# A recurrent layer with a gated feed-forward product: a chunk's state update and scores issued as one run of small matmuls, and a new order for the first 42 products

## The chip, the cores and the metric

The kernel runs on one core of a Trainium2 chip. The metric is the device time of one execution in microseconds (us). A difference is written as a share of the time before.

## The reference

The inputs are r, k, v, w of 4 batches, 8 heads, 768 steps and 48 values per head, a vector u per head, and two weight matrices of 384 x 2048 and 2048 x 384.

```
state = 0                                       # 48 x 48 per batch and head
for t in 768 steps:
    cur   = k[t] (outer) v[t]
    y[t]  = r[t] @ (state + u * cur)
    state = w[t] * state + cur
x   = y as 3072 tokens x 384
h   = x @ w_in
out = (h * sigmoid(1.702 h)) @ w_out
```

## The kernel before, in words

**The recurrence** is worked in 24 chunks of 128 steps, six to a batch, all eight heads at once. Heads stand in pairs: one head of a pair on partitions 0 to 47, the other on 64 to 111, four pairs along the free axis. A chunk is a generator, `chunk(t)`; each `yield` ends a piece, and the order of pieces is set outside. Its pieces before are, with the tiles that they write:

1. S1, S2: two scans of the decay on VectorE (L229, L235, tile `lp`), and the product r*k (`rku`);
2. KQ: decayed keys and queries (L250, L251, tile `kq`);
3. D: for the first eight chunks, matmuls for the u term (`ps_d`, L257); s: its copy, and the old state `sf` scaled (L267);
4. T: the keys transposed on TensorE (`ps_t`, L273) and copied by ScalarE (`kt`, L275); am: the diagonal of the score matrix, eight ScalarE operations (L282);
5. U: the state update. For each half of the chunk, 64 steps, keys times values, 16 small matmuls into two PSUM tiles `ps_u` (L290, L291); VectorE makes from them `mid`, the state at the half (L296; L294 on ScalarE for a batch's first chunk), and the new `sf` (L299). A batch's last chunk needs only the first half;
6. S: the scores, 16 matmuls of keys and queries in blocks of 64 x 64 into two tiles `ps_s`, one for each head of a pair (L306);
7. P: the scores are masked into `am` (L309);
8. Y: scores times values, and half of the state's part (`ps_y`, L319, L330); Z: the other half (L330), and the result split into two f32r halves in `x` (L199, L200). After a group's last chunk, three pairs of small DMAs fill spare rows of `x` (L356).

Each of the 16 matmuls of a piece shows twice in the profile. The tiles `ps_d`, `ps_t`, `ps_u`, `ps_s` and `ps_y` all come from one pool of three PSUM banks, `ps_a`, in turn.

**The feed-forward part** takes four chunks as a group of 512 columns. A task is 128 rows of the hidden layer for a group: a first product g (nine matmuls into `ph`, L368 to L370, the high and low parts of x and w_in), a gelu h (two ScalarE operations L379, L380 and one subtraction `gl` on VectorE, L381), and a second product y (nine matmuls into `po`, L394 to L396). The first group starts before its four chunks are done: its first tasks are cut to 256 columns, chunks 0 and 1 (columns 0 to 2) or 2 and 3 (columns 2 to 4). There are 106 tasks, 86 of them with 512 columns.

**The weights** come in six slices for each matrix; f fetches a slice by DMA, w converts it in four pieces into a high and a low part: two ScalarE operations (L185, L186), two VectorE operations (L188, L191), one on ScalarE (L193), one on VectorE (L195). Even numbers (w0, w2, ...) are slices of w_in (`wih`, `wil`), odd ones of w_out (`woh`, `wol`).

**The order** is written by hand, and every engine takes its instructions in that order. Up to task 42 it stands in the string `RAMP`: a token is a letter (l load, a next piece of a chunk, m a sum of squares on ScalarE, f, w, g, h, y as above, x the fill, u and M small loads) and a number. From task 42 on the list `PARTS` sets it: a row ("a", 4, 1) says that a chunk's next piece stands four tasks after the chunk's beginning, and 0 or 1 says whether it stands before the task's g or between its h and the y of the task two before. Chunks begin four tasks apart.

```python
PARTS = [("a", 0, 0), ("a", 1, 0), ("a", 2, 0), ("m", 2, 0), ("a", 2, 1), ("a", 3, 0), ("m", 3, 0), ("l", 3, 0),
         ("l", 3, 0), ("a", 3, 1), ("a", 4, 0), ("a", 4, 1), ("a", 5, 1), ("a", 5, 1), ("a", 6, 1), ("a", 7, 0), ("x", 7, 0)]
```

Of the kernel before, what the change touches and what calls it, by code (L numbers as in the profile page):

```python
# [14 lines left out]
ALU = mybir.AluOpType  # L15
# [15 lines left out]
NF = DFF // P  # L31
# [28 lines left out]
FIRST = 42
RAMP = """
l0 l1 l0 a0 a0 a0 M a0 a0 l0 m0 a0 a1 a0 a1 a0 f0 l1 a0 a0 f1 a1 m0 a1 a0 w0 a1 a0 a1 l2 m1 w0 a1 f2 a1 w1 a1
a2 a1 a2 a1 l3 a2 w0 m1 a1 m2 a2 w0 a2 a2 x1 w1 m2 a3 w2 w2 w1 g0 a3 a2 h0 f3 w1 g1 l2 a3 w2 m3 a2 w3 a2 f4 l3
w2 g2 a3 w3 a2 a3 h1 m3 h2 w4 f5 g3 a3 a2 w4 a3 a2 y0 y1 w3 a3 a3 f6 g4 a3 w4 w3 a3 w4 w5 a3 h3 l4 y2 h4 w6 g5
y3 x3 w5 h5 y4 g6 w5 w6 f7 g7 w5 h6 a4 h7 g8 l4 w6 g9 a4 f8 y5 h8 y6 w7 y7 h9 g10 w6 y8 h10 y9 w8 g11 g12 a4
w7 h11 h12 w7 y10 w7 g13 y12 a4 f9 h13 w8 g14 y11 a4 l5 w9 h14 f10 w9 m4 a4 y13 g15 a5 g16 h15 a4 y14 f11 a5
h16 g17 w8 w8 y15 g18 l6 h17 a5 w9 h18 y16 a4 w9 g19 g20 w10 l7 a5 h19 y17 w10 m4 a5 a4 y18 w11 w11 l5 y19 m5
h20 w10 a4 w11 g21 w10 a5 a4 w11 h21 a4 a6 a5 a5 m5 y20 a5 g22 l6 a6 a6 y21 m6 a5 a6 h22 a5 a6 a7 a5 a6 a6 y22  # L70
a7 a6 g23 a6 m6 a7 l8 a7 a6 a7 m7 a7 l7 a6 a8 g24 h23 a6 a7 a7 g25 a7 u l8 a8 a7 l9 a8 m7 h24 y23 a7 h25 a7
y24 l9 m8 a8 a8 x7 a9 a9 a9 a8 l10 a8 y25 a8 a9 g26 g27 a8 a9 h26 l10 g28 y26 m8 h27 a9 a8 y27 g29 a8 m9 l11
h28 m9 a8 a9 a10 y28 a9 a10 g30 a9 a9 h29 g31 h30 g32 a10 h31 g33 a9 a9 m10 a10 y29 l11 a10 a11 h32 l12 y30
a10 h33 g34 a11 l12 y31 g35 h34 a11 a10 y32 a11 h35 m10 a10 y33 l13 y34 a10 g36 a10 a11 a10 a10 a11 m11 g37
l13 h36 a12 y35 a12 h37 a11 g38 h38 a11 a11 m11 y36 a12 a11 g39 a12 g40 y37 y38 h39 h40 a11 m12 a11 a12 l14
a12 a13 x11 m12 y39 a12 a12 g41 h41 l14
"""
WIDE = 512
assert sum(CHUNKS) == NT
# [3 lines left out]
def rwkv_ffn_kernel(ctx: ExitStack, tc, wkr, vp, vrk, ub, w_in, w_out, masks, vt, uc, out):  # L83
    nc = tc.nc
    V, A, G, T = nc.vector, nc.scalar, nc.gpsimd, nc.tensor
# [49 lines left out]
    loaded, state, pools = {}, {}, {}  # L135
# [80 lines left out]
    def chunk(t):

        i, col = where[t]
        a, v = loaded[t][:2]
        n, nc_ = NP * CW, NP * C  # L220
        w0, w1 = a[:, 0:n], a[:, 1 : n + 1]
        k = a[:, n + 1 : n + 1 + nc_].rearrange("r (p c) -> r p c", p=NP)
        r = a[:, n + 1 + nc_ :].rearrange("r (p c) -> r p c", p=NP)
        first, final = t % CB == 0, (t + 1) % CB == 0
# [39 lines left out]
        sf = None  # L264
        if not first:
            sf = state[t - 1]
# [15 lines left out]
                A.activation(x_[:, p], same, AF.Copy, scale=s[:, 2 * p + h : 2 * p + h + 1])  # L282
        yield

        blocks = [slice(HB * b, HB * b + HB) for b in range(2)]
        ps = [ps_a.tile([R2, NP, D], F32, tag="psa", name=f"ps_u{b}") for b in range(1 if final else 2)]
        for p in range(NP):
            for b, o in enumerate(ps):

                T.matmul(o[0:HB, p], kt[blocks[b], p, 0:HB], v[blocks[b], 2 * p], start=True, stop=True)  # L290
                T.matmul(o[HB:R2, p], kt[blocks[b], p, HB:R2], v[blocks[b], 2 * p + 1], start=True, stop=True)  # L291
        mid = at.tile([R2, NP, D], F32, tag="mid", name="mid", bufs=2)
        if first:
            A.copy(mid, ps[0])  # L294
        else:
            V.tensor_tensor(mid, ps[0], sf, op=ALU.add)  # L296
        if not final:
            new = state[t] = at.tile([R2, NP, D], F32, tag="sf", name="sf", bufs=2)
            V.tensor_tensor(new, ps[1], mid, op=ALU.add)  # L299
        yield  # L300

        ps = [ps_a.tile([P, NP, HB], F32, tag="psa", name=f"ps_s{h}") for h in range(2)]
        for p in range(NP):
            for b in blocks:
                for h in range(2):
                    T.matmul(ps[h][b, p], kf[head(h), p, b], qf[head(h), p, b], start=True, stop=True)  # L306
# [36 lines left out]
        x = xs[i]  # L343
# [18 lines left out]
    def first_product(j, task):  # L362
        i, c0, c1, f = task
        cs = slice(c0 * C, c1 * C)
        ph = ps_h.tile([P, WIDE], F32, tag="ph", name="ph")[:, 0 : (c1 - c0) * C]
        for c in range(NM):
            h_, l_ = (w[:, f, c * P : (c + 1) * P] for w in (wih, wil))
            T.matmul(ph, h_, xs[i][:, 0, c, cs], start=c == 0, stop=False)  # L368
            T.matmul(ph, h_, xs[i][:, 1, c, cs], start=False, stop=False)  # L369
            T.matmul(ph, l_, xs[i][:, 0, c, cs], start=False, stop=c == NM - 1)  # L370
        parts[j] = ph

    def gelu(j, task):
        i, c0, c1, f = task
        ph, n = parts[j], (c1 - c0) * C
        gf = mo.tile([P, WIDE], F32, tag="gf", name="gf")[:, 0:n]
        gh = mo.tile([P, WIDE], F32R, tag="gh", name="gh", bufs=LAG + 1)[:, 0:n]
        gl = mo.tile([P, WIDE], F32R, tag="gl", name="gl", bufs=LAG + 1)[:, 0:n]
        A.activation(gh, ph, AF.Gelu_apprx_sigmoid, scale=1.0 / W_SCALE)  # L379
        A.activation(gf, ph, AF.Gelu_apprx_sigmoid, scale=1.0 / W_SCALE)  # L380
        V.tensor_tensor(gl, gf, gh.bitcast(F32), op=ALU.subtract)  # L381
        parts[j] = gh, gl
# [27 lines left out]
    with tc.manual_schedule():  # L410
# [16 lines left out]

        def do(token):
# [68 lines left out]
    ps = ps_a.tile([1, 1], F32, tag="psa", name="ps_n")  # L497
# [6 lines left out]
    with tc.If(n < full):  # L504
# [5 lines left out]
        with tc.tile_pool(name="gp", bufs=1) as gp, tc.tile_pool(name="ob", bufs=2) as ob, tc.For_i(0, B, 1) as b:  # L510
            pools["late"] = ob
            xg = [new_x(i) for i in range(2)]
            for p in range(NP):
# [25 lines left out]
                for half in range(2):  # L539
                    x = xg[half]  # L540
# [65 lines left out]
```

## Time and profile before

| | |
|---|---|
| median of 3 runs (lowest to highest) | 551.46 us (551.0 to 554.75) |
| the profiled execution | 551.16 us |
| its span in the profile | 549.6 us |
| TensorE busy | 515.8 us, 94% |
| TensorE's weight loads | 419.7 us, 76% |
| VectorE busy | 282.3 us, 51% |
| ScalarE busy | 277.4 us, 50% |
| GpSimd busy | 32.9 us, 6% |
| HBM read and written | 40.36 and 4.72 MB |

The profile is one execution on the chip. TensorE's matmuls overlap, so a time between two starts says more of their cost than the duration of one. The shares are means over a ramp of some 70 us, in which weights and first chunks are prepared, a long even part, and the last group's products. The profiled execution's own time holds 1.6 us more than its span.

### The profile page before, as it was taken

The page shows a single profiled execution, that of the slowest core. Times are in us where ns is not written, and L with a number is a line of the kernel's source. Part 1 is how long each engine was busy: PE and PEld are TensorE (multiplying, and loading weights), DVE is VectorE, ACT ScalarE, POOL GpSimd, SP SyncE. Part 2 cuts the span into 40 slices and gives each one's busy share as a digit, 9 for nine tenths or more (in the row PEclk, how much of TensorE's full clock was granted, in tenths as well). Part 3 has the DMA queues.
Part 4 walks back from the last instruction along what each step waited for, and adds up shares of the span by engine and source line. Part 5 has one row for each costly group of instructions (what it writes and reads, how often), then busy time and mean ns, then how long its engine had stood idle before and what let it go on. Part 6 is the DMA issues. An engine that isn't in the chain of part 4 may idle for free.

```text
span 549.6 us, 11888 instructions
## 1 busy us (share of the span) xinstructions
PE 515.8 (94%) x5014; PEld 419.7 (76%) x5014; DVE 282.3 (51%) x510; ACT 277.4 (50%) x644; POOL 32.9 (6%) x72
## 2 busy tenths in 40 slices
PE   1776999999999999999999999999999999999993
PEld 1666899877777877777777777777777777888882
DVE  3797899887735453655455445445455422111110
ACT  1787878866653453555345355345355342332221
POOL 4011101000100000100001000001000001000000
PEclk9996999999999999999999999999999999999998
DMA  8958599444642312344122344121440001100001
GB/s 181 242 158 213 93 268 209 95 101 119 166 110 67 80 44 51 94 130 94 37 59 36 111 129 94 42 54 26 121 131 1 1 1 30 44 14 0 1 0 64
DMA packets 17518, 48.30 MB, mean 88 GB/s; under 512 B 3024, under 2 KB 6416, under 8 KB 17456
## 3 DMA queue, kind: packets, MB, share of 16 engines
q1 hardware_dynamic: 14096, 36.02, 25.2%
q0 software_dynamic: 3104, 11.13, 10.2%
q8 instruction: 41, 0.67, 0.6%
q10 hardware_dynamic: 256, 0.30, 0.2%
q14 instruction: 21, 0.17, 0.1%
HBM read 40.36 MB, written 4.72 MB: 82 GB/s over the span
## 4 chain that ended last, share of the span: by engine, by line
PE 92%; DVE 3%; DMA 1%; ACT 1%; issue 1%; SPq 0%; DVEq 0%; ACTq 0%
PE po L394 14%; PE ph L368 13%; PE ph L370 12%; PE ph L369 12%; PE po L396 12%; PE po L395 12%; PE ps_y L330 5%; PE ps_y L319 3%; PE ps_s L306 3%; PE ps_t L273 2%; PE ps_d L257 2%; PE ps_u L290 2%; DMA wkr_t<-in_wkr 1%; PE ps_u L291 1%; DVE st L188 0%
## 5 line engine op out<-in xcount | busy, mean ns | idle before, releaser
L381 DVE TENSOR_TENSOR gl<-gf,gh 128x512 fp32r<-128x512 f32 (+1 forms) x106 | 67.5, 639 | 171.8 <-ACT gf L380 171.6
L379 ACT ACTIVATE gh<-ph 128x512 fp32r<-128x512 f32 (+1 forms) x106 | 59.0, 557 | 171.1 <-PE ph L370 162.7
L394 PE MATMUL po<-gh,woh 128*128 128x512 f32 (+1 forms) x318 | 124.6, 392 | 0.0
L368 PE MATMUL ph<-x,wih 128*128 128x512 f32 (+1 forms) x318 | 123.5, 388 | 1.0 <-DMA x<-x 1.0
L370 PE MATMUL ph<-x,wil 128*128 128x512 f32 (+1 forms) x318 | 120.0, 377 | 0.0
L369 PE MATMUL ph<-x,wih 128*128 128x512 f32 (+1 forms) x318 | 119.9, 377 | 0.0
L396 PE MATMUL po<-gl,woh 128*128 128x512 f32 (+1 forms) x318 | 118.2, 372 | 0.0
L395 PE MATMUL po<-gh,wol 128*128 128x512 f32 (+1 forms) x318 | 118.0, 371 | 0.0
L368 PEld LDWEIGHTS ph<-x,wih 128*128 128x128 f32 x318 | 61.5, 193 | 13.6 <-ACT kt L275 1.3
L370 PEld LDWEIGHTS ph<-x,wil 128*128 128x128 f32 x318 | 61.6, 194 | 11.2
L369 PEld LDWEIGHTS ph<-x,wih 128*128 128x128 f32 x318 | 61.7, 194 | 9.8
L394 PEld LDWEIGHTS po<-gh,woh 128*128 128x128 f32 x318 | 59.9, 189 | 11.6
L396 PEld LDWEIGHTS po<-gl,woh 128*128 128x128 f32 x318 | 60.0, 189 | 11.0
L395 PEld LDWEIGHTS po<-gh,wol 128*128 128x128 f32 x318 | 60.1, 189 | 8.5
L380 ACT ACTIVATE gf<-ph 128x512 f32<-128x512 f32 (+1 forms) x106 | 58.8, 554 | 0.0
L282 ACT ACTIVATE am<-same,s 128x64 f32<-128x64 f32 x192 | 48.6, 345 | 0.3 <-PE ps_y L319 0.2
L199 ACT CAST x<-ps_y 112x256 fp32r<-112x256 f32 x48 | 15.8, 374 | 56.5 <-PE ps_y L330 54.7
L200 DVE TENSOR_TENSOR x<-ps_y,x 112x256 fp32r<-112x256 f32 x48 | 18.3, 418 | 33.7 <-ACT x L199 33.7
L330 PE MATMUL ps_y<-kq,mid 48*48 48x64 f32 x384 | 32.0, 226 | 3.5 <-DVE mid L338 3.5
L330 PEld LDWEIGHTS ps_y<-kq,mid 48*48 48x48 f32 x384 | 25.9, 126 | 9.6 <-DVE mid L338 5.3
L229 DVE TENSOR_TENSOR_SCAN lp<-wkr_t,d1r 112x516 f32<-112x516 f32 x24 | 29.4, 1226 | 5.1 <-DMA wkr_t<-in_wkr 4.9
L235 DVE TENSOR_TENSOR_SCAN lp<-wkr_t,d1f 112x516 f32<-112x516 f32 x24 | 29.4, 1226 | 0.2
(67 smaller groups left out, 543.3 us busy)
## 6 DMA issues: line engine op xcount, KB each, us to landing
wkr_t<-in_wkr SPq DMA_DIRECT2D x23, 385.2 KB, 4.7
wkr_t<-in_wkr POOLq DMA_DIRECT2D x23, 288.9 KB, 5.9
st<-in_w_out SPq DMA_DIRECT2D x6, 1024.0 KB, 9.5
rk_t<-in_vrk SPq DMA_DIRECT2D x16, 384.0 KB, 3.8
v_t<-in_vrk SPq DMA_DIRECT2D x24, 192.0 KB, 5.4
out_t<-ob SPq DMA_DIRECT2D x18, 256.0 KB, 2.2
st<-in_w_in POOLq DMA_DIRECT2D x6, 384.0 KB, 9.7
st<-in_w_in SPq DMA_DIRECT2D x6, 384.0 KB, 8.0
```

The costliest lines, as they stand in the source:

```text
L229: V.tensor_tensor_scan(li.rearrange("r p c -> r (p c)")[:, ::-1], w1[:, ::-1], d1r.rearrange("r p c -> r (p c)")[:, ::-1], 0.0, op0=ALU.mu ...
L282: A.activation(x_[:, p], same, AF.Copy, scale=s[:, 2 * p + h : 2 * p + h + 1])
L330: T.matmul(ps[b][head(h), p], from_[head(h), p], qf[head(h), p, blocks[b]], start=False, stop=p == NP - 1, skip_group_check=True,)
L368: T.matmul(ph, h_, xs[i][:, 0, c, cs], start=c == 0, stop=False)
L369: T.matmul(ph, h_, xs[i][:, 1, c, cs], start=False, stop=False)
L370: T.matmul(ph, l_, xs[i][:, 0, c, cs], start=False, stop=c == NM - 1)
L379: A.activation(gh, ph, AF.Gelu_apprx_sigmoid, scale=1.0 / W_SCALE)
L380: A.activation(gf, ph, AF.Gelu_apprx_sigmoid, scale=1.0 / W_SCALE)
L381: V.tensor_tensor(gl, gf, gh.bitcast(F32), op=ALU.subtract)
L394: T.matmul(o, woh[:, f, ms], gh, start=first, stop=False, skip_group_check=True)
L395: T.matmul(o, wol[:, f, ms], gh, start=False, stop=False, skip_group_check=True)
L396: T.matmul(o, woh[:, f, ms], gl, start=False, stop=f == NF - 1, skip_group_check=True)
```

## The change

A chunk's U and S become one piece: 32 matmuls without another instruction of TensorE between them. The two PSUM tiles of the piece, still named `ps_u`, each hold in one bank the update of one half (columns 0 to 191) and the scores of one head of the pairs (columns 192 to 447). Both users of a tile read the same half of the partitions, and so run on the same half of the array's rows. `mid` and the new `sf` come after the scores in the order. The chunk has 11 pieces instead of 12. In `PARTS` one ("a", 5, 1) goes, and Z and the fill move from ("a", 7, 0) to ("a", 7, 1), behind the task's first product. The order of the first group's tasks and `RAMP` are new: columns 2 to 4 come with tasks 5 to 9 already, and conversions and chunks stand otherwise among them.

```diff
-TASKS = [(0, 0, 2, f) for f in range(5)]
-TASKS += [x for f in range(5) for x in ((0, 0, 2, f + 5), (0, 2, 4, f))]
-TASKS += [(0, 2, 4, f) for f in range(5, 10)] + [(0, 0, 4, f) for f in range(10, NF)]
+TASKS = [(0, c, c + 2, f) for c in (0, 2) for f in range(5)]
+TASKS += [(0, c, c + 2, f) for f in range(5, 10) for c in (0, 2)]
+TASKS += [(0, 0, 4, f) for f in range(10, NF)]
...
-         ("l", 3, 0), ("a", 3, 1), ("a", 4, 0), ("a", 4, 1), ("a", 5, 1), ("a", 5, 1), ("a", 6, 1), ("a", 7, 0), ("x", 7, 0)]
+         ("l", 3, 0), ("a", 3, 1), ("a", 4, 0), ("a", 4, 1), ("a", 5, 1), ("a", 6, 1), ("a", 7, 1), ("x", 7, 1)]
...
-l0 l1 l0 a0 a0 a0 M a0 a0 l0 m0 a0 a1 a0 a1 a0 f0 l1 a0 a0 f1 a1 m0 a1 a0 w0 a1 a0 a1 l2 m1 w0 a1 f2 a1 w1 a1
+l0 a0 l0 M a0 a0 l0 l1 m0 a0 f0 a0 a0 a1 a1 a0 a0 a0 m0 a1 a0 a1 a0 l1 f1 a1 a1 w0 l2 a1 m1 a1 w0 a1 a2 a1 a2
...
         blocks = [slice(HB * b, HB * b + HB) for b in range(2)]
-        ps = [ps_a.tile([R2, NP, D], F32, tag="psa", name=f"ps_u{b}") for b in range(1 if final else 2)]
+        both = [ps_a.tile([P, NP * (D + HB)], F32, tag="psa", name=f"ps_u{i}") for i in range(2)]
+        us = [x[0:R2, 0 : NP * D].rearrange("r (p d) -> r p d", p=NP) for x in both]
+        ps = [x[:, NP * D :].rearrange("r (p c) -> r p c", p=NP) for x in both]
         for p in range(NP):
-            for b, o in enumerate(ps):
+            for b, o in enumerate(us[0 : 1 if final else 2]):
 
                 T.matmul(o[0:HB, p], kt[blocks[b], p, 0:HB], v[blocks[b], 2 * p], start=True, stop=True)
                 T.matmul(o[HB:R2, p], kt[blocks[b], p, HB:R2], v[blocks[b], 2 * p + 1], start=True, stop=True)
+        for p in range(NP):
+            for b in blocks:
+                for h in range(2):
+                    T.matmul(ps[h][b, p], kf[head(h), p, b], qf[head(h), p, b], start=True, stop=True)
         mid = at.tile([R2, NP, D], F32, tag="mid", name="mid", bufs=2)
         if first:
-            A.copy(mid, ps[0])
+            A.copy(mid, us[0])
         else:
-            V.tensor_tensor(mid, ps[0], sf, op=ALU.add)
+            V.tensor_tensor(mid, us[0], sf, op=ALU.add)
         if not final:
             new = state[t] = at.tile([R2, NP, D], F32, tag="sf", name="sf", bufs=2)
-            V.tensor_tensor(new, ps[1], mid, op=ALU.add)
-        yield
-
-        ps = [ps_a.tile([P, NP, HB], F32, tag="psa", name=f"ps_s{h}") for h in range(2)]
-        for p in range(NP):
-            for b in blocks:
-                for h in range(2):
-                    T.matmul(ps[h][b, p], kf[head(h), p, b], qf[head(h), p, b], start=True, stop=True)
+            V.tensor_tensor(new, us[1], mid, op=ALU.add)
         yield
```

The changed kernel is one line shorter ahead of the chunk, so that most of its lines have numbers one lower (L394 becomes L393), and the scores are its L297, the masking its L308.

On TensorE, in the even part, chunk 15's state update before ends in these rows, where 3469 and 3470 number the two tiles, and a second product follows:

```order
L290 MATMUL ps_u_3469<-v_t,kt 64x48
L291 MATMUL ps_u_3469<-v_t,kt 48x48
L290 MATMUL ps_u_3470<-v_t,kt 64x48
L291 MATMUL ps_u_3470<-v_t,kt 48x48
L394 MATMUL po_2986<-gh,woh 128x512
L395 MATMUL po_2986<-gh,wol 128x512
L396 MATMUL po_2986<-gl,woh 128x512
```

Its scores begin nine second and nine first matmuls later, in two tiles of their own:

```order
L368 MATMUL ph<-x,wih 128x512
L369 MATMUL ph<-x,wih 128x512
L370 MATMUL ph<-x,wil 128x512
L306 MATMUL ps_s_3519<-kq 64x64
L306 MATMUL ps_s_3520<-kq 64x64
```

In the changed kernel the same place on TensorE reads as follows, with the scores (L297) in the tiles of the update:

```order
L292 MATMUL ps_u_3441<-v_t,kt 64x48
L293 MATMUL ps_u_3441<-v_t,kt 48x48
L292 MATMUL ps_u_3442<-v_t,kt 64x48
L293 MATMUL ps_u_3442<-v_t,kt 48x48
L297 MATMUL ps_u_3441<-kq 64x64
L297 MATMUL ps_u_3442<-kq 64x64
```

The scores moved ahead by a second and a first product, and stand directly behind the update.

On VectorE, in the ramp, these rows follow the write of chunk 1 into x before the change; `wil` is the last piece of the first slice of w_in, `st` and `c` are a slice's second piece, `lp` and `rku` belong to chunk 3:

```order
L200 TENSOR_TENSOR x<-ps_y_344,x 112x4x64
L195 TENSOR_TENSOR wil<-c,wih 128x1024
L260 COPY s<-ps_d 128x8
L267 TENSOR_TENSOR sf<-sf,lp 112x192
L188 SCALAR_TENSOR_TENSOR st<-st 128x1024
L191 SCALAR_TENSOR_TENSOR c<-c,st 128x1024
L229 SCALAR_TENSOR_TENSOR lp<-wkr_t,d1r 112x516
```

In the changed kernel the same place on VectorE has:

```order
L199 TENSOR_TENSOR x<-ps_y_328,x 112x4x64
L259 COPY s<-ps_d 128x8
L266 TENSOR_TENSOR sf<-sf,lp 112x192
L187 SCALAR_TENSOR_TENSOR st<-st 128x1024
L190 SCALAR_TENSOR_TENSOR c<-c,st 128x1024
L228 SCALAR_TENSOR_TENSOR lp<-wkr_t,d1r 112x516
L232 RECIPROCAL d1f<-lp 112x4
L234 SCALAR_TENSOR_TENSOR lp<-wkr_t,d1f 112x516
L241 TENSOR_TENSOR rku<-wkr_t 112x512
L194 TENSOR_TENSOR wil<-c,wih 128x1024
L302 TENSOR_TENSOR mid<-ps_u_434,sf 112x192
```

The last piece of w_in's first slice moved from directly behind the write of x to behind the next slice's second piece and both scans of chunk 3.

More of the change, by code (lines that the diff above doesn't have):

```diff
@@ L63 @@
 RAMP = """
-l0 l1 l0 a0 a0 a0 M a0 a0 l0 m0 a0 a1 a0 a1 a0 f0 l1 a0 a0 f1 a1 m0 a1 a0 w0 a1 a0 a1 l2 m1 w0 a1 f2 a1 w1 a1
[L65 to L73, printed above, removed]
@@ L74 @@
-a10 h33 g34 a11 l12 y31 g35 h34 a11 a10 y32 a11 h35 m10 a10 y33 l13 y34 a10 g36 a10 a11 a10 a10 a11 m11 g37
-l13 h36 a12 y35 a12 h37 a11 g38 h38 a11 a11 m11 y36 a12 a11 g39 a12 g40 y37 y38 h39 h40 a11 m12 a11 a12 l14
-a12 a13 x11 m12 y39 a12 a12 g41 h41 l14
+l0 a0 l0 M a0 a0 l0 l1 m0 a0 f0 a0 a0 a1 a1 a0 a0 a0 m0 a1 a0 a1 a0 l1 f1 a1 a1 w0 l2 a1 m1 a1 w0 a1 a2 a1 a2
+a2 w1 w0 a1 a2 a2 m1 a2 w1 m2 a2 l3 l2 a3 f2 a3 m2 w1 x1 w0 a2 a3 a3 w2 a2 f3 g0 w1 m3 l3 f4 a3 h0 g1 h1 a3 a2
+y0 w3 y1 w2 w3 l4 a3 f5 a2 a3 a3 w2 m3 a3 w2 w3 a3 x3 g2 h2 w3 g3 h3 g4 y2 w4 a4 y3 f6 h4 w4 g5 w5 g6 h5 y4 w5
@@ new lines @@
+w4 g7 h6 w4 h7 a4 w5 y5 w5 g8 h8 w6 g9 y6 g10 y7 h9 y8 g11 f7 w6 w7 w7 h10 y9 g12 h11 w6 w6 g13 w7 l4 w7 h12
+y10 h13 y11 g14 a4 f8 f9 w8 y13 g15 h14 y12 w9 l5 g16 w8 a4 h15 w9 w8 m4 w8 y14 y15 h16 g17 w9 a4 a4 g18 a5
+h17 a5 f10 y16 h18 g19 g20 a5 a4 y17 w9 h19 w10 y18 w10 m4 f11 a4 l5 a5 a4 h20 l6 w11 w10 y19 l7 w11 g21 h21
+m5 y20 g22 a5 w10 m5 a6 w11 a5 l6 a4 w11 a4 a5 g23 a6 a5 a5 y21 h22 a6 a6 m6 a5 a6 a7 l8 a5 a7 a6 y22 a6 a7 a6
+m6 g24 a7 a6 l7 a7 h23 a7 a6 a6 a7 a7 a7 g25 l9 a7 h24 l8 a7 m7 a8 h25 y23 u a8 a8 x7 m7 y24 y25 l9 g26 m8 a8
@@ L77 @@
+h26 g27 h27 g28 a8 a8 y26 a8 y27 a9 a9 h28 g29 l10 y28 a8 g30 a9 m8 h29 a8 m9 g31 h30 a9 a9 l10 a9 a8 a10 a9
+a8 y29 g32 y30 h31 y31 a10 a9 h32 l11 a9 g33 g34 l11 m9 a10 m10 h33 y32 g35 m10 a10 a10 a9 h34 a9 a10 l12 g36
+a11 a11 y33 h35 a10 g37 a11 h36 y34 m11 h37 a10 a10 g38 a11 a11 g39 m11 a12 a10 l12 a12 a10 a12 a11 a12 a11
+a12 y35 h38 y36 a11 l13 a11 a12 h39 g40 a11 m12 l13 a11 x11 y37 l14 m12 a12 y38 g41 y39 h40 a12 a13 h41 l14
 """
@@ L285, in chunk @@
         blocks = [slice(HB * b, HB * b + HB) for b in range(2)]
-        ps = [ps_a.tile([R2, NP, D], F32, tag="psa", name=f"ps_u{b}") for b in range(1 if final else 2)]
+        both = [ps_a.tile([P, NP * (D + HB)], F32, tag="psa", name=f"ps_u{i}") for i in range(2)]
+        us = [x[0:R2, 0 : NP * D].rearrange("r (p d) -> r p d", p=NP) for x in both]
+        ps = [x[:, NP * D :].rearrange("r (p c) -> r p c", p=NP) for x in both]
         for p in range(NP):
-            for b, o in enumerate(ps):
+            for b, o in enumerate(us[0 : 1 if final else 2]):
                 T.matmul(o[0:HB, p], kt[blocks[b], p, 0:HB], v[blocks[b], 2 * p], start=True, stop=True)
                 T.matmul(o[HB:R2, p], kt[blocks[b], p, HB:R2], v[blocks[b], 2 * p + 1], start=True, stop=True)
-        mid = at.tile([R2, NP, D], F32, tag="mid", name="mid", bufs=2)
-        if first:
-            A.copy(mid, ps[0])
[L295 to L298, printed above, removed]
-            V.tensor_tensor(new, ps[1], mid, op=ALU.add)
-        yield
-        ps = [ps_a.tile([P, NP, HB], F32, tag="psa", name=f"ps_s{h}") for h in range(2)]
         for p in range(NP):
@@ L306, in chunk @@
                     T.matmul(ps[h][b, p], kf[head(h), p, b], qf[head(h), p, b], start=True, stop=True)
+        mid = at.tile([R2, NP, D], F32, tag="mid", name="mid", bufs=2)
+        if first:
+            A.copy(mid, us[0])
+        else:
+            V.tensor_tensor(mid, us[0], sf, op=ALU.add)
+        if not final:
+            new = state[t] = at.tile([R2, NP, D], F32, tag="sf", name="sf", bufs=2)
+            V.tensor_tensor(new, us[1], mid, op=ALU.add)
         yield
```

## The prediction, made before the changed kernel was run

> **What bounds the kernel now.** I read the page's chain first, then the busy time by stretches, then the timeline of TensorE (PE) and of VectorE (DVE) at the places that the change touches.
>
> ```profile
> PE 92%; DVE 3%; DMA 1%; ACT 1%; issue 1%; SPq 0%; DVEq 0%; ACTq 0%
> ```
>
> ```profile
> 40.00:50.00 10.00, 4.87 (x79) 4.46 (x78) 9.83 (x14) 8.47 (x22) 0.00 (x0) 0.68 0.94 260
> 50.00:60.00 10.00, 9.34 (x165) 8.50 (x164) 5.85 (x14) 8.25 (x18) 1.56 (x3) 0.80 0.91 174
> ...
> 70.00:100.00 30.00, 30.00 (x272) 29.52 (x271) 28.34 (x43) 24.79 (x56) 2.12 (x4) 1.00 1.00 224
> 100.00:200.00 100.00, 98.09 (x1200) 78.50 (x1199) 62.85 (x121) 55.33 (x137) 4.65 (x9) 1.00 0.41 102
> 200.00:460.00 260.00, 259.68 (x2524) 203.73 (x2523) 126.28 (x244) 126.04 (x307) 9.82 (x19) 1.00 0.26 64
> ```
>
> The columns of the stretches are length, PE, PE's weight loads, DVE, ScalarE (ACT), GpSimd, PE's granted clock, DMA. From 70 us on PE never rests (30.00 of 30, 98.09 of 100, 259.68 of 260), with DVE and ACT half idle after 200 us: there each us that PE saves is a us of the end. Before 70 us DVE fills its time (9.83 of 10) and PE waits. So the change has two prices: PE time per chunk after 70 us, and the order of DVE's queue before.
>
> **Part 1: one run instead of two.** What one run of small matmuls costs PE is read from the starts: from the last large matmul before it to the second large one after it, less two plain steps. All of these lie among 128x512 matmuls.
>
> ```profile
> 204.38 0.40 PE L369 MATMUL ph<-x,wih 128*128 128x512 f32 x1
> 204.61 0.40 PE L370 MATMUL ph<-x,wil 128*128 128x512 f32 x1
> 204.94 0.25 PE L290 MATMUL ps_u<-v_t,kt 64*64 64x48 f32 x1
> ...
> 205.44 0.65 PE L306 MATMUL ps_s<-kq 48*64 48x64 f32 x29
> 206.01 0.50 PE L394 MATMUL po<-gh,woh 128*128 128x512 f32 x1
> 206.34 0.40 PE L395 MATMUL po<-gh,wol 128*128 128x512 f32 x1
> ```
>
> This is chunk 11, whose state update and scores happen to follow each other before the change too. A plain step is 204.61 - 204.38 = 0.23. The joint run costs 206.34 - 204.61 - 0.46 = 1.27. Chunk 10 has the two apart:
>
> ```profile
> 187.97 0.39 PE L396 MATMUL po<-gl,woh 128*128 128x512 f32 x1
> ...
> 188.67 0.29 PE L290 MATMUL ps_u<-v_t,kt 64*64 64x48 f32 x4
> ...
> 189.22 0.39 PE L395 MATMUL po<-gh,wol 128*128 128x512 f32 x1
> ...
> 192.88 0.39 PE L396 MATMUL po<-gl,woh 128*128 128x512 f32 x1
> 193.20 0.70 PE L306 MATMUL ps_s<-kq 48*64 48x64 f32 x32
> 193.82 0.49 PE L368 MATMUL ph<-x,wih 128*128 128x512 f32 x1
> 194.16 0.40 PE L369 MATMUL ph<-x,wih 128*128 128x512 f32 x1
> ```
>
> Update: 189.22 - 187.97 - 0.46 = 0.79. Scores: 194.16 - 192.88 - 0.46 = 0.82. Apart 1.61, joint 1.27: **0.34 saved**. Of it the edges are (193.20 - 192.88 - 0.23) + (194.16 - 193.82 - 0.23) = 0.09 + 0.11 = 0.20; the rest is the tail of the update that runs beside the first scores. Chunk 11 is a last chunk of its batch and updates from one half only. The other chunks put the second half on the other half of the array, so the run should hardly lengthen; but if it did, down to the edges alone, 0.20 is left. I take **0.35**, 0.01 above the row, because the matmuls behind an edge are for a while also slightly slower (0.23 against 0.227).
>
> [...]
>
> How often: chunks 0 to 3 and 11 have update and scores side by side already. Of the other 19, all run after 96 us, under a busy PE: 19 x 0.35 = **6.65 us**; bounds 19 x 0.20 = 3.8 and, if some eight slower steps behind each edge count in full, 19 x 0.38 = 7.2.
>
> Nothing new is late there: in 200 to 460 us DVE and ACT are half idle, the transposed keys that the run needs were issued a product earlier, and mid and the new state, which now wait for the scores too (both sit in the same two tiles), are next needed by the output's matmuls two tasks later.
>
> One place loses: in chunk 7 the run follows the output of chunk 6 with only three buffers for all of it, so it waits for a cast and a subtraction:
>
> ```profile
> L199 ACT CAST x<-ps_y 112x256 fp32r<-112x256 f32 x48 | 15.8, 374 | 56.5 <-PE ps_y L330 54.7 <-PE ps_u L291 1.0 <-PE ps_y L319 0.9
> L200 DVE TENSOR_TENSOR x<-ps_y,x 112x256 fp32r<-112x256 f32 x48 | 18.3, 418 | 33.7 <-ACT x L199 33.7
> ```
>
> 0.374 + 0.418 = **+0.8 us**, once.
>
> The last part of a chunk (second state matmuls, split into x, fill DMAs) now stands after a task's first product, one product (9 x 0.23 = 2.1) later.
>
> ```profile
> 379.06 0.25 PE L330 MATMUL ps_y<-kq,mid 48*48 48x64 f32 x1
> 381.54 1.53 POOL L356 DMA_DIRECT2D x<-x  x3 [26.93 <-issue]
> ```
>
> ```profile
> DMA to landing us min/median/max: 2.2/2.8/4.1
> ```
>
> Its fills are issued by 4.0 us after the part starts (381.54 + 1.53 - 379.06) and land 4.1 later at most: 8.1. Two gelus now stand ahead on ACT, at an estimated 0.6 each (the cast of half as many columns takes 0.374): 9.3. The next group's first product begins after the part itself (0.6, as many matmuls as the scores, 193.82 - 193.20), three products (6.3) and the run (1.3): 8.2, and reads the last piece six steps (1.4) on: 9.6. **Nothing**, with 0.3 to spare at the worst landing and 1.6 at the median one. SP's loads for chunk t+3, past which the fills are moved, were issued at least a product before them.
>
> **Part 2: the ramp.** PE starts the first products when x of chunks 0 and 1 and the first slice of w_in are there.
>
> ```profile
> 32.81 0.76 DVE L200 TENSOR_TENSOR x<-ps_y,x 112x256 fp32r<-112x256 f32 x2 [0.40 <-ACT x L199]
> 33.48 1.22 DVE L195 TENSOR_TENSOR wil<-c,wih 128x1024 fp32r<-128x1024 f32 x1
> ...
> 36.00 0.55 PE L368 MATMUL ph<-x,wih 128*128 128x256 f32 x1 [1.00 <-DMA x<-x]
> ...
> 63.93 0.76 DVE L200 TENSOR_TENSOR x<-ps_y,x 112x256 fp32r<-112x256 f32 x2 [0.21 <-ACT x L199]
> ...
> 96.46 0.26 PE L290 MATMUL ps_u<-v_t,kt 64*64 64x48 f32 x1
> ```
>
> Up to chunk 1's write of x (33.6) DVE has the same work in both orders, so I leave it there, within the one wait that the new order of loads can remove, 2.9 us, either way:
>
> ```profile
> DVE rku L242 <- DMA wkr_t<-in_wkr: 2.9, 1, 2.9
> ```
>
> ```profile
> L229 DVE TENSOR_TENSOR_SCAN lp<-wkr_t,d1r 112x516 f32<-112x516 f32 x24 | 29.4, 1226 | 5.1 <-DMA wkr_t<-in_wkr 4.9
> L191 DVE SCALAR_TENSOR_TENSOR c<-c,st 128x1024 int32<-128x1024 int32 x12 | 14.7, 1226 | 0.4
> L195 DVE TENSOR_TENSOR wil<-c,wih 128x1024 fp32r<-128x1024 f32 x6 | 7.3, 1214 | 0.0
> L250 DVE TENSOR_TENSOR kq<-wkr_t,lp 112x512 f32<-112x512 f32 x24 | 16.4, 682 | 0.0
> L381 DVE TENSOR_TENSOR gl<-gf,gh 128x256 fp32r<-128x256 f32 x20 | 8.2, 418 | 1.1 <-ACT gf L380 0.9
> ```
>
> The small operations without a row here (s, mid, state, fewer columns than L200's 256) I estimate at 0.35 each, below its 0.418, and a mask of 256 columns at 0.44. Then, in the new order, DVE has chunk 2's s (0.5), the two operations of w1 (2.45), both scans of chunk 3 (3.3 with product and reciprocal), and only then w0's last (1.2): 33.6 + 7.5 = 41.1. The first product starts **5.1 us later**. Then stand mid and state of chunk 2, keys and queries of chunk 3, masks, w1's last, s, two gl, and w2's and w3's two (0.7 + 1.4 + 0.9 + 1.2 + 0.5 + 0.8 + 4.9 = 10.4), and x of chunk 2, mid, state and masks of chunk 3, w2's last, x of chunk 3 (4.7): 56.2, with 2.7 for PE's answers in between 58.9. Before, that x ended at 64.7: **5.8 us earlier**. What follows has to be fed by both engines up to the update of chunk 4, at 96.46 before. PE then has 17 first and 15 second products of 256 columns:
>
> ```profile
> 85.31 0.28 PE L369 MATMUL ph<-x,wih 128*128 128x256 f32 x1
> 85.43 0.28 PE L370 MATMUL ph<-x,wil 128*128 128x256 f32 x1
> ```
>
> 32 x 9 x 0.12 + 1.1 for chunk 4's small ones = 35.7 from 58.0 on (w2's last): 93.7. DVE has six conversions (6 x 3.66), 15 gl (6.3), chunk 4's scans and keys and chunk 5's first scan (4.7): 33.0 from 58.9: 91.9. Two queues that full wait for each other; I take 2 us: 95.7, a gain of **0.8**, bounds 3.7 (no start wait) and a loss of 2.1 (the 2.9 the other way).
>
> The wait of the scores for mid, which the change takes away, is worth nothing of its own: what was late then is DVE, with the conversions.
>
> ```profile
> PE ps_s L306 <- DVE mid L296: 4.6, 3, 3.6
> ```
>
> **The sum.** -6.65 + 0.8 - 0.8 = -6.65. The profiled execution took 551.16 (span 549.6), so 544.5; the median of the three runs is 0.3 above it: **544.8**. A difference under 1% (5.5 us) is about what a measurement cannot tell from no change.
>
> **Rivals.** *Only the edges are saved* (0.20 a chunk; for it: joint runs of update and scores with both halves are not in the trace under a full clock; against: chunk 11): 544.8 + 2.85 = 547.7, chance 0.14. *The ramp gains what its middle gains*: if DVE does not hold PE back after 58.9, nearly all of the 5.8 stays, 544.8 - 5.0 = 539.8; against it stands DVE's 28.34 of 30 busy in 70 to 100; 0.14. *Fills late*: if the 0.3 of slack is missed by 1 us at each of four group ends, 548.8; 0.06. *The slow one*: PE runs the first products at half rate.
>
> ```profile
> 36.35 0.42 PE L369 MATMUL ph<-x,wih 128*128 128x256 f32 x1
> 36.57 0.42 PE L370 MATMUL ph<-x,wil 128*128 128x256 f32 x1
> ```
>
> 0.22 a step here against 0.12 at 85 us, and the stretches grant 0.68 and 0.80: 3.2 + 2.0 us lost, 10.4 us at half clock. The new ramp puts PE in short pieces between 41 and 58. If the half clock then lasts another 10.4 us from 58 on, 5.2 are lost, and y0, y1 and chunk 3's run, at half rate on DVE's way to x, cost 2.2 + 1.3 more: 544.8 + 8.7 = 553.5. It decides from 6.65 us of loss in the ramp on; 0.09. That the run is not joined at all is excluded by the order of instructions.
>
> **How the numbers follow.** The forecast has 0.53 (541.5 to 548 by itself); 0.04 is left for something else. The range of 8 in 10 takes in the ramp's gain and the edges alone, and leaves out the half clock: 539.5 to 550.5. Faster by over 1% (under 546.0): the gain in the ramp and most of the forecast, 0.57; slower by over 1% 0.04; the rest 0.39.
>
> **What would show it.** The run of chunk 15 or so should cost 1.25 to 1.35 by the same starts, and PE have no idle time after 70 us. The first product should start near 41, x of chunk 3 end near 59, the update of chunk 4 follow the same 32 products by 95 to 96.5. I am wrong if the run costs 1.5, if PE waits for x<-x at a group's start, or if the clock is still at half after 58 us.

## The result, and the profile after

| | before | changed |
|---|---|---|
| median (lowest to highest) of 14 executions each | 552.12 us (550.67 to 554.75) | 548.39 us (546.66 to 551.57) |
| ratio, with its 95% interval | | 0.9933 (0.9918 to 0.9948) |
| the profiled execution, its span | 551.16, 549.6 us | 551.57, 550.0 us |
| TensorE busy in it | 515.8 us | 510.3 us |

The change saves 0.67%, 3.7 us, of the 6.65 that were forecast. The profiled execution of the changed kernel is the slowest of its 14, and no faster than the one before, although TensorE (PE) has 5.5 us less to do in it. That makes it useful: what PE gained must stand in it as idle time. It is called the first profile below; a second one of the changed kernel was taken later. The chain of waits, and then the busy time of the same stretches as in the prediction:

```profile
PE 89%; DMA 3%; DVE 3%; issue 2%; ACT 1%; POOL 0%; DVEq 0%; ACTq 0%; POOLq 0%
```

```profile
40.00:50.00 10.00, 8.03 (x83) 7.84 (x84) 8.16 (x16) 8.07 (x16) 0.48 (x1) 1.00 1.03 281
50.00:60.00 10.00, 5.82 (x138) 5.40 (x138) 6.57 (x10) 6.51 (x17) 0.00 (x0) 0.74 0.32 113
70.00:100.00 30.00, 28.86 (x238) 28.41 (x237) 26.31 (x33) 24.05 (x48) 3.16 (x6) 1.00 1.02 223
100.00:200.00 100.00, 96.70 (x1116) 79.61 (x1115) 67.38 (x127) 62.33 (x154) 4.67 (x9) 0.98 0.40 98
200.00:460.00 260.00, 259.37 (x2663) 207.30 (x2661) 128.00 (x254) 125.31 (x308) 10.32 (x20) 1.00 0.28 69
```

PE's share of the chain fell from 92 to 89%. PE's work came earlier in 40 to 50 us (8.03 us where it was 4.87) and is missing in 50 to 60 (5.82 where it was 9.34). VectorE (DVE), which had no rest in 40 to 50 (9.83), works 8.16 there, and 6.57 in the ten us after it (5.85 before). From 70 to 200 us PE rests 1.14 and 3.30 us, where it rested 0 and 1.91. From 200 us on it rests 0.6 us of 260 (0.3 before). So the even part has no new waits, and time was lost ahead of it. The whole ramp in one row, before and then after, has DVE in its third busy time (after PE and PE's weight loads):

```profile
0.00:62.00 62.00, 39.21 (x587) 35.32 (x589) 44.26 (x72) 40.29 (x89) 11.69 (x31) 0.92 0.83 191
```

```profile
0.00:62.00 62.00, 35.60 (x581) 32.41 (x581) 40.44 (x69) 35.51 (x81) 12.04 (x29) 0.94 0.73 174
```

DVE has done 3.8 us less by 62 us, and PE 3.6. Where DVE stood still shows its timeline:

```profile
22.97 0.35 DVE L266 TENSOR_TENSOR sf<-sf,lp 112x192 f32<-112x192 f32 x1
25.76 0.36 DVE L302 TENSOR_TENSOR mid<-ps_u,sf 112x192 f32<-112x192 f32 x1 [2.44 <-PE ps_u L297]
...
26.50 1.22 DVE L187 SCALAR_TENSOR_TENSOR st<-st 128x1024 int32<-128x1024 int32 x1
...
34.90 0.73 DVE L199 TENSOR_TENSOR x<-ps_y,x 112x256 fp32r<-112x256 f32 x2
...
41.74 1.22 DVE L194 TENSOR_TENSOR wil<-c,wih 128x1024 fp32r<-128x1024 f32 x1
...
56.99 0.36 DVE L302 TENSOR_TENSOR mid<-ps_u,sf 112x192 f32<-112x192 f32 x1 [1.74 <-PE ps_u L297]
```

At 23.3 DVE waits 2.44 us for the run of chunk 1, with the conversion of the first weight slice (26.50) behind that wait. Before, the conversion stood ahead of `mid`, in what would have been the wait:

```profile
23.68 1.22 DVE L188 SCALAR_TENSOR_TENSOR st<-st 128x1024 int32<-128x1024 int32 x1
...
26.08 0.35 DVE L296 TENSOR_TENSOR mid<-ps_u,sf 112x192 f32<-112x192 f32 x1
```

The joined run of the even part, chunk 15's, by the prediction's measure:

```profile
287.07 0.39 PE L369 MATMUL ph<-x,wil 128*128 128x512 f32 x1
287.39 0.25 PE L292 MATMUL ps_u<-v_t,kt 64*64 64x48 f32 x1
...
288.48 0.50 PE L393 MATMUL po<-gh,woh 128*128 128x512 f32 x1
288.81 0.39 PE L394 MATMUL po<-gh,wol 128*128 128x512 f32 x1
```

288.81 - 287.07 - 0.46 = 1.28, inside the 1.25 to 1.35 that were given for it.

### The profile page after: what moved, and what is told of

The parts are those of the page before. It is cut to its first block, busy times and chain, and to the rows that moved or that the text cites. A ratio compares the mean times of both kernels' runs of the same rounds, so it can differ in the third digit from the quotient of the medians.

```text
span 550.0 us, 11921 instructions
## 1 busy us (share of the span) xinstructions
PE 510.3 (93%) x5014; PEld 421.7 (77%) x5014; DVE 280.9 (51%) x510; ACT 276.2 (50%) x644; POOL 34.3 (6%) x72
## 3 DMA queue, kind: packets, MB, share of 16 engines
q1 hardware_dynamic: 14096, 36.02, 25.4%
## 4 chain that ended last, share of the span: by engine, by line
PE 89%; DMA 3%; DVE 3%; issue 2%; ACT 1%; POOL 0%; DVEq 0%; ACTq 0%; POOLq 0%
PE po L393 13%; PE ph L367 12%; PE ph L369 12%; PE ph L368 12%; PE po L395 12%; PE po L394 12%; PE ps_y L329 5%; PE ps_y L318 3%; PE ps_u L297 2%; PE ps_t L272 2%; DMA st<-in_w_out 2%; PE ps_u L292 2%; PE ps_d L256 2%; DMA hm<-in_masks 1%; DVE st L187 1%
## 5 line engine op out<-in xcount | busy, mean ns | idle before, releaser
L393 PE MATMUL po<-gh,woh 128*128 128x512 f32 (+1 forms) x318 | 123.4, 388 | 0.9 <-ACT gh L378 0.9
L367 PE MATMUL ph<-x,wih 128*128 128x512 f32 (+1 forms) x318 | 121.1, 381 | 0.0
L368 PE MATMUL ph<-x,wih 128*128 128x512 f32 (+1 forms) x318 | 119.7, 376 | 0.0
L394 PE MATMUL po<-gh,wol 128*128 128x512 f32 (+1 forms) x318 | 118.4, 372 | 0.0
L393 PEld LDWEIGHTS po<-gh,woh 128*128 128x128 f32 x318 | 60.3, 190 | 12.6 <-ACT gh L378 1.1
L394 PEld LDWEIGHTS po<-gh,wol 128*128 128x128 f32 x318 | 60.5, 190 | 9.3
L379 ACT ACTIVATE gf<-ph 128x512 f32<-128x512 f32 (+1 forms) x106 | 58.9, 556 | 0.0
L125 POOL DMA_DIRECT2D wkr_t<-in_wkr x23 | 12.1, 526 | 256.7 <-DVE kq L250 250.7
```

The source lines that it names most:

```text
L393: T.matmul(o, woh[:, f, ms], gh, start=first, stop=False, skip_group_check=True)
L394: T.matmul(o, wol[:, f, ms], gh, start=False, stop=False, skip_group_check=True)
```

## The experiments

My theory after this reading: the join brings its forecast or more, and the new order of the first 42 tasks, which was to bring 0.8 us, costs some 4. The rival: the order is neutral and the join is worth only 3.7. "Before" ran beside each set: 551.63 us (15 executions) beside the first four, 551.29 (11) beside the others.

| | median us | ratio to before (95%) | run of chunk 4 starts at |
|---|---|---|---|
| before | | | 96.46 |
| joined run, old order | 545.32 | 0.9888 (0.9864 to 0.9912) | 95.84 |
| the same, a DVE gap filled | 544.62 | 0.9873 (0.9853 to 0.9893) | 95.47 |
| separate pieces, new order | 566.13 | 1.0252 (1.0228 to 1.0276) | 107.26 |
| changed, last part ahead of the product | 548.66 | 0.9944 (0.9925 to 0.9963) | 105.93 |
| changed, split ahead of weights | 548.04 | 0.9928 (0.9912 to 0.9944) | 106.29 |
| changed, first weights earlier | 545.95 | 0.9898 (0.9869 to 0.9928) | 103.41 |
| changed once more | 547.77 | 0.9929 (0.9910 to 0.9949) | 105.64 |
| separate tiles side by side, old order | 570.60 | 1.0337 (1.0302 to 1.0373) | |

The last column is read from the first row of that run in each profile; in the changed kernel's first profile it starts at 106.71. In the new order four more products stand ahead of it (three of 256 columns, one of 512: 27 x 0.12 + 9 x 0.23 = 5.3 us), so that 105.64 there means 100.3 on the scale of before, and 106.71 means 101.4.

**The join without the new order.**

```diff
 # against the changed kernel: TASKS and RAMP of before,
 # each chunk's token for the scores left out; RAMP begins:
-l0 a0 l0 M a0 a0 l0 l1 m0 a0 f0 a0 a0 a1 a1 a0 a0 a0 m0 ...
+l0 l1 l0 a0 a0 a0 M a0 a0 l0 m0 a0 a1 a0 a1 a0 f0 l1 a0 f1 ...
```

> The joined run and the later last part, with the first 42 tasks in the order of before (in that order each chunk's separate scores piece is left out, and the run stands where the state update stood). Theory A (the join is worth more than forecast, about 0.43 us for each of 19 chunks = 8.2 us, and the new order of the first tasks gives some 4.5 us of it back): 552.1 - 8.2 + 0.8 for the wait in chunk 7 = 544.7, below the changed kernel by 3 to 4 us; first product near 36, PE idle in all near 25 us. Theory B (the new order costs nothing and the join is worth only the 3.7 us that the change brought): 548.4, like the changed kernel.

545.32 us, 6.2 below before (interval 4.8 to 7.5) and beside my 544.7. Against the changed kernel (0.9888 / 0.9933) it is 0.45% faster, 2.5 us, with an interval from 0.9 to 4.1. The first product starts at 35.48, and PE is idle for 27.2 us in all (I had said near 25), where the changed kernel had 31.5 and before 25.4 (sums over PE's timeline, from the span's start to the last matmul). Theory A holds; the rival's 548.4 lies outside the interval (544.1 to 546.8). Only the order differs between this kernel and the changed one, so its price is the 2.5 us of the medians. The profiles show more: chunk 4's run comes 4.5 us later with the new order (100.3 against 95.84), and the spans are 4.6 apart with the second profile (546.8 against 542.2). But this profiled execution is the fastest of its six.

One wait of the prediction turns up here, at another chunk than it said:

```profile
PE ps_u L297 <- DVE x L199: 0.8, 1, 0.8
```

**The order without the join.**

```diff
 # against before: TASKS and RAMP of the changed kernel,
 # behind each chunk's update a second token for its scores
-... a0 a0 a0 m0 a1 a0 a1 a0 l1 f1 ...
+... a0 a0 a0 a0 m0 a1 a0 a1 a0 l1 f1 ...
```

> The new order of the first 42 tasks, but state update and scores as two pieces in tiles of their own, one directly after the other in that order, and from task 42 on the places of before. Theory A: the order alone costs 4 to 5 us, so 556 to 557; PE idle before 62 us some 4 us more than before. Theory B: within 1 us of 552.1. If the separate tiles make the new order wait for PSUM buffers more often than the joined ones, it comes out above 557 and tells less of the order.

566.13 us, 14.5 above before, more than either theory gave: the case in which it tells less. Up to the run of chunk 4 it is at 107.26, 1.6 behind the changed kernel, so most of the delay up to there belongs to the order, not to the joined tiles. In the profile that is 5.5 of the 12.3 us by which its span is longer than before. Most of the rest belongs to the tiles:

```profile
PE ps_s L306 <- DVE mid L296: 4.3, 4, 2.4
```

That is PE's waits from 100 us on: scores directly behind an update find no fourth buffer and wait until `mid` has been read out. Behind the longest of them, 2.43 us, the granted clock is at a half for 3.4 us, by estimate (half of that time) some 1.7 us more. With the pieces side by side in tiles of their own the new order costs more than its own price; other places for the scores in it were not tried.

**The last part of a chunk back in its place.**

```diff
-("a", 6, 1), ("a", 7, 1), ("x", 7, 1)]
+("a", 6, 1), ("a", 7, 0), ("x", 7, 0)]
```

> The changed kernel, but from task 42 on a chunk's last part (second state matmuls, split, fills) stands ahead of a task's first product, as before, not behind it. Theory A: of the 0.43 us a chunk about 0.1 is that the last part now stands directly ahead of the next chunk's transposes and so saves an edge on TensorE; without it 11 chunks x 0.1 = 1.1 us more than the changed kernel, four tasks take 20.2 instead of 20.1 us, fills land 2 us earlier and nobody gains by it. Theory B: the whole 0.43 is the joined run; then no difference, and the four tasks stay at 20.1.

In time no difference can be measured (0.9944 against 0.9933 and 0.9929). The trace can tell: these are the first rows of the runs of chunks 13 and 23, before, in the changed kernel, and here.

```profile
241.86 0.25 PE L290 MATMUL ps_u<-v_t,kt 64*64 64x48 f32 x1
...
448.18 0.25 PE L290 MATMUL ps_u<-v_t,kt 64*64 64x48 f32 x1
```

```profile
247.21 0.25 PE L292 MATMUL ps_u<-v_t,kt 64*64 64x48 f32 x1
...
449.14 0.25 PE L292 MATMUL ps_u<-v_t,kt 64*64 64x48 f32 x1
```

```profile
244.68 0.25 PE L292 MATMUL ps_u<-v_t,kt 64*64 64x48 f32 x1
...
447.30 0.25 PE L292 MATMUL ps_u<-v_t,kt 64*64 64x48 f32 x1
```

Ten chunks take 206.32, 201.93 and 202.62 us. The changed kernel saves 0.44 a chunk: **0.37 is the joined run, 0.07 the place of the last part**, which in the changed kernel stands directly ahead of the next chunk's transposes (`ps_t`, 302.83 behind 302.69) and so next to other small matmuls. Theory A's 0.1 was of the right size, and too small to be seen in the time.

**Chunk 2's split ahead of two weight slices.**

```diff
-y0 w3 y1 w2 w3 l4 a3 f5 a2 a3 a3 ...
+y0 a2 w3 y1 w2 w3 l4 a3 f5 a3 a3 ...
```

> The changed kernel with one piece moved in the first 42 tasks: the last part of chunk 2 (second state matmuls, split into x) is given out directly behind the first second product, ahead of the four VectorE passes of the third and fourth weight slices, behind which it now stands. Theory A: the run of chunk 3 needs two of three PSUM buffers and waits 4.3 us for that split's reads; with it moved the run starts at once, chunk 3's x is there some 3 us earlier, and the time falls by 2 to 3 us, to about 546. Theory B: VectorE's queue is as long as before, what it does not do earlier it does later, and x of chunk 3 comes less than 1 us earlier; 548.4 within 0.8.

548.04: no gain, theory B. In the changed kernel PE waited for this split (`ps_u` for `x`) and then for chunk 3's masks, as its waits up to 70 us say:

```profile
PE ps_y L318 <- DVE am L308: 7.4, 3, 4.1
...
PE ps_u L292 <- DVE x L199: 2.5, 1, 2.5
```

Here the second of these is gone and the first is longer by more than it:

```profile
PE ps_y L318 <- DVE am L308: 10.8, 3, 5.1
```

DVE says why:

```profile
52.10 0.76 DVE L199 TENSOR_TENSOR x<-ps_y,x 112x256 fp32r<-112x256 f32 x2 [2.04 <-ACT x L198]
```

DVE now waits 2.04 us for the split's cast, a wait that the four conversion passes had filled, and ahead of it 1.14 instead of 0.50 for TensorE. The conversions begin 3 us later (52.77, where it was 49.69), chunk 3's masks stand behind them as before, and chunk 3's x ends at 63.7, not earlier than the 63.2 and 62.8 of the changed kernel's two profiles. The edit took a wait from PE and opened one on DVE.

**The first weight slice into the gap.**

```diff
-... a0 m0 a1 a0 a1 a0 l1 f1 a1 a1 w0 l2 a1 m1 a1 w0 a1 ...
+... a0 m0 a1 a0 w0 a1 a0 l1 f1 a1 w0 a1 l2 a1 m1 a1 a1 ...
```

> The changed kernel with the first weight slice moved in the first 42 tasks: its two ScalarE passes stand ahead of chunk 1's keys' bonus matmuls and its two VectorE passes ahead of chunk 1's transposes, where VectorE now waits 2.44 us for the run of chunk 1. Theory A (the new order's price is VectorE waiting early, which is never made up while VectorE is the busiest): the first product starts some 2.4 us earlier, near 41, x of chunk 3 2 us earlier, and the time falls by about 2 us to 546. Theory B (an early gain only turns into a later wait, as when the split of chunk 2 was moved): first product earlier, but the time within 0.8 of 548.2.

545.95, 1.8 below the changed kernel of the same set (0.9898 against 0.9929; the interval of that, 3.6 below to 0.2 above, takes in zero), about what theory A said; the time alone does not settle it. The trace is plainer. DVE first, then PE:

```profile
22.85 0.35 DVE L266 TENSOR_TENSOR sf<-sf,lp 112x192 f32<-112x192 f32 x1
23.12 1.22 DVE L187 SCALAR_TENSOR_TENSOR st<-st 128x1024 int32<-128x1024 int32 x1
...
25.65 0.36 DVE L302 TENSOR_TENSOR mid<-ps_u,sf 112x192 f32<-112x192 f32 x1
...
59.85 0.76 DVE L199 TENSOR_TENSOR x<-ps_y,x 112x256 fp32r<-112x256 f32 x2 [0.47 <-ACT x L198]
```

```profile
41.16 0.56 PE L367 MATMUL ph<-x,wih 128*128 128x256 f32 x1
...
103.41 0.25 PE L292 MATMUL ps_u<-v_t,kt 64*64 64x48 f32 x1
```

The same places of the unaltered kernel, in the profile that was taken beside it:

```profile
62.03 0.76 DVE L199 TENSOR_TENSOR x<-ps_y,x 112x256 fp32r<-112x256 f32 x2 [0.47 <-ACT x L198]
```

```profile
43.42 0.56 PE L367 MATMUL ph<-x,wih 128*128 128x256 f32 x1
...
105.64 0.25 PE L292 MATMUL ps_u<-v_t,kt 64*64 64x48 f32 x1
```

The gap is gone, and everything behind it is earlier by nearly its length: the first product by 2.26, chunk 3's x by 2.18, chunk 4's run by 2.23. One gap, at 23 us, is over half of what the new order costs: 2.23 of the 3.9 us by which chunk 4's run is later than before.

**A second gap, in the old order.**

```diff
 # against the joined run with the old order
-... g3 a3 a2 w4 a3 a2 y0 y1 ...
+... g3 a3 w4 a2 a3 a2 y0 y1 ...
```

> The joined run with the first tasks in the order of before, and one piece moved there: the two VectorE passes of the fifth weight slice stand ahead of, not behind, the small copy with which the output of chunk 2 waits for TensorE; VectorE has 2.85 us idle at that place. Theory A: VectorE's gap is filled, x of chunks 2 and 3 come some 2.3 us earlier, TensorE's products follow, and the time falls by 1 to 2 us below 545.3. Theory B: the next wait takes it back, 545.3 within 0.8.

544.62, 0.7 below the joined run with the old order, which is no measurable difference (0.9873 against 0.9888), and chunk 4's run 0.37 earlier: theory B. Most of DVE's gap of 2.85 us came back at two later places:

```profile
55.42 0.76 DVE L199 TENSOR_TENSOR x<-ps_y,x 112x256 fp32r<-112x256 f32 x2 [1.42 <-ACT x L198]
58.20 0.36 DVE L302 TENSOR_TENSOR mid<-ps_u,sf 112x192 f32<-112x192 f32 x1 [2.02 <-PE ps_u L297]
```

The first of these waits was not there without the edit, and the second was 1.05. There DVE answers PE, and PE answers DVE, within one chunk; earlier work only makes DVE wait earlier. It has the lowest median of all, 3.1 us (0.9873 / 0.9929, interval 1.5 to 4.6) below the changed kernel of its set.

**Side by side, in separate tiles.**

```diff
 # against before; from chunk 12 on
-("a", 4, 1), ("a", 5, 1), ("a", 5, 1), ("a", 6, 1)
+("a", 4, 1), ("a", 4, 1), ("a", 5, 1), ("a", 6, 1)
 # and the scores of chunk 12 at the end of RAMP
-y39 a12 a12 g41
+y39 a12 a12 a12 g41
```

> The kernel before with one entry of its table moved: from chunk 12 on the scores' matmuls stand directly behind the state update's, each still in tiles of its own (four in all, with three buffers). Theory A (the shared tiles are what the gain needs): the second tile of the scores waits until mid has been read out of the first tile of the update, about 0.4 us of PE a chunk, which eats the 0.38 us of the edges; within 1 us of before, and TensorE shows an idle time between update and scores in each chunk. Theory B (the neighbourhood alone is the gain): 11 chunks x 0.38 = 4 us less than before, four tasks in 20.17 us.

570.60, 19.3 us above before. The mechanism is theory A's, its price more than three times as large:

```profile
286.50 0.39 PE L370 MATMUL ph<-x,wil 128*128 128x512 f32 x1
...
287.32 0.29 PE L306 MATMUL ps_s<-kq 48*64 48x64 f32 x2
289.06 0.69 PE L306 MATMUL ps_s<-kq 48*64 48x64 f32 x30 [1.45 <-DVE mid L296]
289.68 0.74 PE L394 MATMUL po<-gh,woh 128*128 128x512 f32 x1
```

```profile
288.05 0.69 DVE L381 TENSOR_TENSOR gl<-gf,gh 128x512 fp32r<-128x512 f32 x1 [2.44 <-ACT gf L380]
288.66 0.35 DVE L296 TENSOR_TENSOR mid<-ps_u,sf 112x192 f32<-112x192 f32 x1
```

The second tile of the scores waits for `mid`, and `mid` stands on DVE behind the `gl` of the product just done, which waits for its gelu. I had priced `mid` alone. The pauses, eight of 1.44 to 1.45 us and two shorter ones (1.22, 0.66), sum to 13.5 us. The clock adds to it. Stretches of 1 us around this pause, with the granted clock third from the end:

```profile
289.00:290.00 1.00, 0.94 (x31) 0.88 (x32) 0.90 (x3) 0.00 (x0) 0.00 (x0) 0.88 0.00 0
290.00:291.00 1.00, 1.00 (x3) 0.80 (x3) 1.00 (x2) 0.00 (x0) 0.00 (x0) 0.50 0.00 0
...
292.00:293.00 1.00, 1.00 (x4) 0.81 (x3) 0.00 (x0) 0.00 (x0) 0.00 (x0) 0.50 0.00 0
293.00:294.00 1.00, 1.00 (x5) 0.79 (x5) 0.00 (x0) 0.00 (x0) 0.00 (x0) 0.91 0.00 0
```

The clock is at a half for some 3.4 us, in which large matmuls start every 0.43 us (289.68 to 293.20) instead of every 0.23; half of that time is 1.7 us, an estimate of the cost. So it is after four of the eight pauses, 6.8 us in all. So with three buffers and DVE's order as it is, the neighbourhood pays only with shared tiles. A fourth buffer, or `mid` ahead of `gl` on DVE, was not tried. Chunks 17 and 23, which update from one half only, need one tile less and show no such pause.

**The changed kernel again.**

> The changed kernel once more, unaltered, to have it and a second profile beside these: 548.2 within 1, so that the joined run with the old order of the first tasks stays 2 to 4 us below it. If in this execution TensorE's 1.4 us pause in the output of chunk 7 is there again, it belongs to the program; the wait of 0.9 us at 95 us for a late slice of w_out need not come back.

547.77 (547.17 to 548.34). Its span is 546.8, 3.2 us below the first profile's. The wait at 95 us, in which PE waits for a gelu and ScalarE for the DMA of a slice of w_out, was 0.91 us of PE in the first profile and is 0.39 here. The pause in chunk 7's output came back as 0.9:

```profile
PE ps_y L329 <- issue: 0.9, 1, 0.9
```

"Issue" means that the profile shows nothing that PE waited for. The pause is at this place in all five profiles that have the joined run and the new order or a version of it (0.9 to 1.4 us), and not in those with the old order, so it belongs to the program. In the first profile the pause is 1.42 us, and there the granted clock is at a half for some 3.4 us behind it. The pause, that clock (an estimated 1.7 us) and the wait at 95 us make 2.7 of the 3.2 us between the two profiles; whether they make the spread of the other executions (546.7 to 551.6) is not shown, and the cause of the pause was not tried.

## Why the prediction was right or wrong

- **One run instead of two: right, and a little low.** 0.35 a chunk was forecast, within 0.20 to 0.38; measured 0.37, and 0.07 more from the last part's new place, which the prediction put at nothing. It had asked whether the fills come too late there, not what the matmuls meet. Joined run and wait were -6.65 + 0.8 = -5.85; with the old order of the first tasks they measure -6.2. The rivals of the edges alone (547.7) and of late fills (548.8) come closer to the measured 548.4 than the forecast, and neither is what happened: 0.20 a chunk is the wrong number, and after 62 us no fill was waited for. A gain of the right size with a loss that has nothing to do with it looks the same in the time.
- **The number: in the range, by its width.** 548.4 lies outside the band of the forecast by itself (541.5 to 548), and the case that came, less than 1% either way, had 0.39. That the range held is no sign that the sum was right: one term of it had the wrong sign.
- **More than the edges.** The edges are 0.20; the 0.37 measured with the last part in its old place is more. The prediction put the rest down to the update's tail that runs beside the first scores. In chunk 15's run the two do overlap: the first scores start at 287.80, the update's last matmuls at 287.83. What that is worth by itself no run tried, and what makes an edge cost its 0.1 us none shows. The update's second half did not lengthen the run: 1.28 in chunk 15 with both halves, 1.27 in chunk 11 with one.
- **The wait in chunk 7: wrong place, right size.** It does not appear there, nor anywhere in the changed kernel after 70 us; the joined run in the old order has it in chunk 5, at 0.84. Chunk 7 has the pause without a releaser instead, 0.9 to 1.4.
- **Fills: right.** These are all of PE's waits from 62 to 470 us in the first profile, and none is for `x`:

```profile
PE ps_y L329 <- DVE mid L337: 2.5, 8, 0.3
PE ps_y L329 <- issue: 1.4, 1, 1.4
PE po L393 <- ACT gh L378: 0.9, 1, 0.9
PE po L395 <- DVE gl L380: 0.2, 1, 0.2
```

- **The ramp: the step that failed.** A gain of 0.8 was forecast with bounds of 3.7 and a loss of 2.1; the loss is about 2.5 in the medians and, against before, 3.9 in the second profile (100.3 against 96.46) and 4.9 in the first. Three links of the sum, by that profile: first product 41.1 forecast, 43.4 measured; x of chunk 3 58.9 and 62.8 (62.03 + 0.76); chunk 4's run, on the scale of before, 95.7 and 100.3. The first link failed at "up to chunk 1's write of x DVE has the same work in both orders, so I leave it there". The same work, but not the same waits: it ended at 34.90 + 0.73 = 35.6 in the first profile, not 33.6, since the conversion that had filled a wait now stood behind it; with the conversion back in the wait it ended at 33.1 (32.38 + 0.74). The sum from there on, 7.5 us, was 7.3 by the trace. The second link took another 2.3 to 2.5 too long: where I had put 2.7 us for all of PE's answers, DVE waits 6.1 from 42.96 (41.74 + 1.22) to 62.5, in five pieces of which the 1.74 above is one; its own work was about 1 us less than I had counted. Of the 2.3 to 2.5, some 1.9 is an estimate of what the half clock costs there: from the run of chunk 3 to `mid` it takes 2.02 (54.97 to 56.99), and from the output's first matmul to x 3.83 (58.63 to 62.46); at full clock, in the joined run with the old order, 1.21 (57.20 to 58.41) and 2.76 (60.06 to 63.30, less a pause of 0.48).
- **The half clock after 58 us** came as the rival said, though not at its price. It is granted from 55 to 65 us, where before it was 44 to 53.5: by half of PE's busy time under it, an estimated 4.0 us lost (up to 70 us) where it was 3.9. The steps of the products with 256 columns say the same: some 30 of them take 0.21 to 0.22 us in either kernel, also where the profile still gives the clock as 1.00 (from 36 us before, from 44 changed). So the half clock moved with the ramp instead of being added to it. But where it lies now it slows the way to chunk 3's x, the 1.9 us above; for that the rival had 2.2 + 1.3.
- **No idle PE after 70 us: wrong** by 0.9 and 0.4 us at 95 us in the two profiles and by the pause at 140 us in both.

## What to carry to other kernels

When an order is rewritten, add up the waits of the engine that is fullest, not its work: look for each place where it waits for another engine and ask what stood in that wait before and what stands there now. A gap is worth its length if what fills it is needed later anyway and the gap is not the answer to the engine's own last result; two edits of the same kind here brought chunk 4's run forward by 2.2 us and 0.4. And a large change should be split before it is judged: the join without the new order gained 6.2 us, the order on top of it lost 2.5, and together they read as a gain of 3.7 that is easily taken for a weak join.

## What the runs showed of the hardware

The granted clock fell to a half behind some pauses of PE and not behind others of the same length. With separate tiles side by side it fell after four of eight pauses of 1.44 to 1.45 us, each time for some 3.4 us, and not after the other four. In the new order without the join it fell after 2.43 us; in the changed kernel's first profile it fell after 1.42 us, and not after the 0.9 of the second, nor after 1.39 at the same place in the kernel with the split ahead of the weights. What decides between equal pauses was not shown.
